# Token mix 2 in four steps between the pairs of channel product 1, and token mix 1 only inside channel product 2

## The chip, the cores and the metric

The kernel runs on one core of a Trainium2 chip. The metric is the device time of one execution in microseconds (us). The core's engines work in parallel, each through its own instructions in order: PE (TensorE, the matrix products), DVE (VectorE), ACT (ScalarE), POOL (GpSimd) and SP (SyncE, which here only issues transfers). Semaphores order them against each other.

## The reference

Eight batches of 4096 tokens by 192 channels, all in fp32. Cut to what matters:

```
w = softmax(weight, axis=-1)                              # 8 heads, 7 taps; a head is 24 channels
x = causal depthwise convolution of x with w              # along the tokens, per head
u = x + (relu(x^T @ w_tok1) @ w_tok2)^T                   # w_tok1 4096 x 256, w_tok2 256 x 4096
out = u + relu(u @ w_ch1) @ w_ch2                         # w_ch1 192 x 1536, w_ch2 1536 x 192
```

## The kernel before, in words

Work is done in five groups of batches: two of one batch (called single here) and three of two batches (pair groups). Group 0 is batch 0, group 1 batch 1, group 2 batches 2 and 3, and so on. Each batch has eight tiles of 512 tokens. A tile-batch, 64 of them in all, is numbered here as a *row*, from 1 on: rows 1 to 8 are batch 0, rows 9 to 16 batch 1, rows 17 to 32 group 2, rows 33 to 48 group 3.

Four kinds of matrix product share PE:

- **Token mix 1** (`mix`, line 861): `x^T @ w_tok1`, summed over all 4096 tokens of a group in two banks of the accumulator memory (`ps_a`). A group's tokens come in units called q, of two token rows each; a q needs `xhl` (the convolved tokens, split into a high and a low part by ACT, line 824, and DVE, line 828; two buffers) and a part of `w_tok1` (`t1`, loaded by SP and in group 2 split as well, lines 808 and 812).
- **Token mix 2** (`mix2`, line 1030): the next tile's `u`, four banks of `ps_x`, added to the convolved tokens on DVE (lines 1041 and 1042 for a single batch, 1051 for a pair).
- **Channel product 1** (`channel1`, line 1211): six pairs p of 18 matmuls. Each pair fills two banks of `ps_x`, which ACT (`hh`, line 1268) and DVE (`hl`, line 1269) read out.
- **Channel product 2** (`channel2`, line 1286): four banks of `ps_x`, read out by DVE (`osb`, lines 1298 and 1299).

`ps_x` has six banks in rotation. The operands stand in high and low parts, and three products of parts make one exact product. A matmul uses 64 of the 128 rows of the PE array, and two that stand next to each other run at the same time on the two halves, into different banks. Mix 1, mix 2 and product 2 need both halves for every bank, so they run in steps: halves 0 and 1 of the operands into two banks, and then the halves swapped:

```
SHARES = (0, 1), (2, 3), (1, 0), (3, 2)
```

Between a step and its swap `part_ends` (line 422) has ACT copy two zeros into the end of a bank: PE's next matmul into that bank waits for ACT, and ACT waited for PE's last one. I call it the handshake.

While a group's tiles run through mix 2 and both channel products, the next group is prepared in the background: its convolution (`taps`: DVE line 737, the first of seven taps on ACT), its loads and splits, and its mix 1. Class `Background` sets the order. It holds streams of items with a cost, a lag and a gate, and two clocks, `bg.pe` and `bg.dve`. At each `bg.fg(pe, dve, after)` in the code of the foreground the PE clock is advanced, and the items that are due, by these clocks, are written out at that place. What is left when a group ends is forced (`bg.finish`), and `bg.require(tag)` forces the items up to a tag and sets the PE clock to the later of the two. The clocks are a plan: on the chip each engine runs through its row as fast as its semaphores let it.

After mix 2 the next `u` must be transposed for the next product 1. Up to row 10 PE does that inside product 2. Later DVE transposes blocks of 32 x 32 (lines 1044 and 1052), and `blocks_sent` moves the blocks by 16 transfers, eight from SP's queue and eight from POOL's (line 1126). `parted_single` or `parted` then splits the result (ACT lines 1136, 1157 and 1162, DVE lines 1142 and 1159), and the next product 1 starts. SP's queue carries in the same order the loads of the raw tokens (`raw`, line 725), of `t1` (lines 789 to 802), of `w_tok2` (`t2`, line 979) and of `u` (line 986). From about 1320 us on there is no background left (rows 41 to 64, called quiet here).

Of the kernel before, what the change touches and what calls it, by code (L numbers as in the profile page):

```python
# [34 lines left out]
class Background:  # L35
# [112 lines left out]
def conv_mixer_kernel(ctx: ExitStack, tc: tile.TileContext, x, weight, w_tok1, w_tok2, w_ch1, w_ch2, out):  # L148
# [14 lines left out]
    MJ = 2  # L163
# [257 lines left out]
    def part_ends(ps):  # L421
        nc.scalar.copy(out=ps[0:1, TT - 2:TT], in_=seen)  # L422

# [278 lines left out]
    def stage1(gi, pools):  # L702
# [138 lines left out]

        def mix(q2, q, step):
            st = states[q2]
            n = q2 * (RB // MJ) + q
            if step == 0:
                st["full", q] = bg.full
            st["chunk", q] = bg.chunk
# [7 lines left out]
            else:  # L855
                kcs = (0, 1) if (n + step) % 2 == 0 else (1, 0)
# [8 lines left out]
                if step == 0:  # L865
                    part_ends(accs[kcs[1]])
# [3 lines left out]
        last_q = RB // MJ - 1  # L870
        def loaded(q2, part):
# [60 lines left out]
        for q2 in range(NS):  # L932
# [75 lines left out]
    def mix2(gi, q, t2, u, turned=None):  # L1008
        nb = len(GROUPS[gi])
        n = nb * D  # L1010
# [7 lines left out]
        if nb == 1:  # L1018
            prods = [(kc, r, h1[:, kc, :2 - r, :n], (2 - r) * D) for kc in range(KC) for r in range(2)]
        else:  # L1020
            prods = [(kc, r, h1[:, kc, v, :n], n) for kc in range(KC) for r, v in ((0, 0), (0, 1), (1, 0))]
        pss = {}
        for step, js in enumerate(SHARES):
            for j in js:
                if step < 2:
                    pss[j] = ps_x.tile([P, TT], F32, name="ps_x")
            for i, (kc, r, v, m) in enumerate(prods):
                for k, j in enumerate(js):
                    ks = half_rows(k)
                    nc.tensor.matmul(  # L1030
                        out=pss[j][:, :m], lhsT=lhs(kc, r, j)[ks], rhs=v[ks], start=step < 2 and i == 0,
                        stop=step > 1 and i == len(prods) - 1,
                    )
            if step < 2:
                part_ends(pss[js[1]])
            bg.fg(570 if nb == 1 else 1060, 0 if step < 2 else 1320 if nb == 1 else 1200, 200)
            for j in sorted(js) if step > 1 else ():
                ps = pss[j]
                if nb == 1:
# [3 lines left out]
                    if turned is not None:  # L1043
                        nc.vector.transpose(
                            out=turned[:, :D // QB, j * QB:(j + 1) * QB], in_=two.rearrange("p (n e) -> p n e", e=QB)
                        )
                        bg.dve += 380
                else:
                    uj = u[:, j]
# [535 lines left out]
```

## Time and profile before

| | us |
|---|---|
| three runs | 2056.75, 2057.18, 2061.10 (median 2057.18) |
| the profiled execution | 2053.17 |
| its span | 2051.4 |
| PE busy in the span | 2008.7 |
| DVE, ACT, POOL busy | 1370.7, 807.8, 219.1 |

The profiled execution is 4.0 us faster than the median of the runs. Its mean granted PE clock is 0.997 of full speed. The profile gives busy time by engine, groups of instructions by source line with the idle time before them and what ended it, waits, the chain of work that ended last, and a timeline of every instruction.

### The profile page before, as it was taken

How to read it: one execution, taken by the hardware profiler on the slowest of the kernel's cores; microseconds unless marked ns; L12 is line 12 of the kernel's file. 1: busy time of each engine (PE TensorE's matmuls, PEld its weight loads, DVE VectorE, ACT ScalarE, POOL GpSimd, SP SyncE). 2: the span in 40 equal slices, each digit the busy share in tenths (PEclk: the TensorE clock that was granted, in tenths of full speed). 3: DMA queues.
4: the chain of work that ended last, by engine and by line, in shares of the span. 5: the costliest groups of instructions: out<-in, count | busy, mean ns of one | idle time of the engine just before them, and what ended most of it. 6: DMA issues, size and time to landing. Idle time of an engine off the chain costs nothing.

```text
span 2051.4 us, 52173 instructions
## 1 busy us (share of the span) xinstructions
PE 2008.7 (98%) x22452; PEld 1889.9 (92%) x22452; DVE 1370.7 (67%) x2675; ACT 807.8 (39%) x1562; POOL 219.1 (11%) x385
## 2 busy tenths in 40 slices
PE   9999999998999999999999999999999999999999
PEld 8888999997989998998998989999999999999998
DVE  8888989888858879768745785444454444454443
ACT  5677534433333434334333343332332233333322
POOL 0000000021211011111111001111110111001110
PEclk9999999999999999999999999999999999999999
DMA  9955445656445777266634274322332333333320
GB/s 301 312 166 185 144 133 175 177 144 187 135 133 135 189 190 179 75 153 168 168 76 114 78 221 116 83 70 54 84 77 75 84 80 79 76 76 83 77 54 17
DMA packets 285237, 262.67 MB, mean 128 GB/s; under 512 B 189136, under 2 KB 233040, under 8 KB 285008
## 3 DMA queue, kind: packets, MB, share of 16 engines
q1 hardware_dynamic: 263280, 185.27, 33.6%
q0 software_dynamic: 21728, 74.08, 12.7%
q8 instruction: 177, 2.90, 0.6%
q14 instruction: 52, 0.43, 0.1%
HBM read 146.31 MB, written 71.30 MB: 106 GB/s over the span
## 4 chain that ended last, share of the span: by engine, by line
PE 76%; DVE 9%; DMA 6%; ACT 4%; SPq 3%; issue 1%; POOL 1%; ACTq 0%; DVEq 0%
PE ps_x L1211 34%; PE ps_x L1286 31%; PE ps_a L861 5%; PE ps_x L1030 4%; DVE xc L737 3%; DMA dec_raw<-in_moe_w_tok_dram 2%; DVE hl L1269 2%; SPq L1126 2%; DMA other<-own_hi 1%; DMA raw<-in_x_dram 1%; ACT own_hi L1157 1%; ACT other L1162 1%; DVE own_hi L1052 1%; POOL other L1126 1%; DVE u L1051 1%
## 5 line engine op out<-in xcount | busy, mean ns | idle before, releaser
L1286 PE MATMUL ps_x<-w,hh 64*128 64x384 f32 x5856 | 860.6, 357 | 0.3 <-DVE hl L1269 0.3
L1286 PE MATMUL ps_x<-w,hl 64*128 64x192 f32 x5856 | 831.7, 247 | 0.0
L1286 PEld LDWEIGHTS ps_x<-w,hl 64*128 64x128 f32 x5856 | 738.1, 188 | 0.1
L1286 PEld LDWEIGHTS ps_x<-w,hh 64*128 64x128 f32 x5856 | 734.2, 184 | 1.7 <-DVE hl L1269 0.8
L1268 ACT ACTIVATE hh<-ps_x 128x512 fp32r<-128x512 f32 x744 | 403.6, 594 | 565.8 <-PE ps_x L1211 565.7
L1269 DVE SCALAR_TENSOR_TENSOR hl<-ps_x,hh 128x512 fp32r<-128x512 f32 x744 | 477.1, 685 | 204.6 <-ACT hh L1268 203.6
L737 DVE SCALAR_TENSOR_TENSOR xc<-raw,cw,xc 128x384 f32<-128x384 f32 (+1 forms) x768 | 383.5, 562 | 18.6 <-ACT xc L735 18.5
L1211 PE MATMUL ps_x<-other,w_hi 64*128 64x512 f32 x1296 | 342.1, 390 | 12.6 <-ACT other L1162 12.6
L1211 PE MATMUL ps_x<-own_hi,w_hi 64*128 64x512 f32 x1440 | 338.8, 396 | 10.0 <-ACT own_hi L1136 8.8
L1211 PE MATMUL ps_x<-own_hi,w_lo 64*128 64x512 f32 x1440 | 331.6, 390 | 0.0
L1211 PE MATMUL ps_x<-own_lo,w_hi 64*128 64x512 f32 x1440 | 330.9, 390 | 0.0
L1211 PEld LDWEIGHTS ps_x<-other,w_hi 64*128 64x128 f32 x1296 | 235.5, 184 | 38.4 <-ACT other L1162 16.6
L1298 DVE TENSOR_TENSOR osb<-ps_x,u 128x192 f32<-128x192 f32 x244 | 85.6, 351 | 266.1 <-PE ps_x L1286 266.1
L1211 PEld LDWEIGHTS ps_x<-own_hi,w_hi 64*128 64x128 f32 x1440 | 216.0, 185 | 29.0 <-ACT own_hi L1136 10.2
L1211 PEld LDWEIGHTS ps_x<-own_hi,w_lo 64*128 64x128 f32 x1440 | 221.8, 186 | 18.2
L1211 PEld LDWEIGHTS ps_x<-own_lo,w_hi 64*128 64x128 f32 x1440 | 220.5, 185 | 18.7 <-ACT own_lo L1075 0.4
L422 ACT COPY ps_x<-seen 1x2 f32<-1x2 f32 x198 | 30.1, 152 | 393.1 <-PE ps_x L1286 331.3
L1211 PE MATMUL ps_x<-other,w_lo 64*128 64x512 f32 x648 | 182.8, 388 | 0.0
L1030 PE MATMUL ps_x<-h,t 64*128 64x384 f32 (+1 forms) x1408 | 134.6, 327 | 2.1 <-DVE hl L1269 1.8
L1030 PEld LDWEIGHTS ps_x<-h,t 64*128 64x128 f32 x1408 | 128.0, 184 | 5.2 <-DVE hl L1269 3.7
L1211 PEld LDWEIGHTS ps_x<-other,w_lo 64*128 64x128 f32 x648 | 119.4, 184 | 11.8
L861 PE MATMUL ps_a<-xhl,t 64*128 64x384 f32 x1080 | 123.6, 337 | 5.3 <-ACT ps_a L422 3.0
(176 smaller groups left out, 1826.4 us busy)
## 6 DMA issues: line engine op xcount, KB each, us to landing
raw<-in_x_dram SPq DMA_DIRECT2D x56, 672.0 KB, 8.1
t<-t2d SPq DMA_DIRECT2D x64, 512.0 KB, 5.9
u<-xcd SPq DMA_DIRECT2D x62, 384.0 KB, 7.5
xcd<-xc POOLq DMA_DIRECT2D x28, 768.0 KB, 7.8
t<-t1p SPq DMA_DIRECT2D x32, 512.0 KB, 5.0
out_dram<-osb POOLq DMA_DIRECT2D x34, 384.0 KB, 3.6
out_dram<-osb SPq DMA_DIRECT2D x29, 384.0 KB, 2.8
t2d<-stage SPq DMA_DIRECT2D x16, 512.0 KB, 4.4
```

The costliest lines, as they stand in the source:

```text
L422: nc.scalar.copy(out=ps[0:1, TT - 2:TT], in_=seen)
L737: nc.vector.scalar_tensor_tensor(out=dst, in0=src, scalar=cw[:, h, k:k + 1], in1=dst, op0=ALU.mult, op1=ALU.add)
L861: nc.tensor.matmul(out=accs[kcs[k]][:, :nb * D], lhsT=w[ks], rhs=x[ks], start=first and step == 0 and i == 0, stop=last and step == 1 and ...
L1030: nc.tensor.matmul(out=pss[j][:, :m], lhsT=lhs(kc, r, j)[ks], rhs=v[ks], start=step < 2 and i == 0, stop=step > 1 and i == len(prods) - 1,)
L1051: nc.vector.tensor_tensor(out=uj, in0=v, in1=uj, op=ALU.add)
L1052: nc.vector.transpose(out=turned[:, :, j * QB:(j + 1) * QB], in_=uj.rearrange("p c b d -> p (c b d)").rearrange("p (n e) -> p n e", e=QB),)
L1126: queue.dma_start(out=f32(home[q * QB:(q + 1) * QB, :, i * P:(i + 1) * P]), in_=blocks[i * QB:(i + 1) * QB, q % (2 * nb)],)
L1211: nc.tensor.matmul(out=ps, lhsT=w1[w][rows, t[h][2][c], p * P:(p + 1) * P], rhs=t[h][v][rows, c], start=a and n == 0, stop=z and n == len( ...
L1268: nc.scalar.activation(out=h["hh", f], in_=ps, func=AF.Relu)
L1269: nc.vector.scalar_tensor_tensor(out=h["hl", f], in0=ps, scalar=0.0, in1=f32(h["hh", f]), op0=ALU.max, op1=ALU.subtract)
L1286: nc.tensor.matmul(out=pss[j][:, :m], lhsT=h[part, f][ks, j * P:(j + 1) * P], rhs=w2[ks, f, :m], start=step < 2 and n == 0 and part == "hh ...
L1298: nc.vector.tensor_tensor(out=rows(osb[:, j]), in0=rows(ps[:, :D]), in1=tokens(u, i)[:, j], op=ALU.add)
```

## The change

Mix 2 is no longer one block behind product 1. It returns a function for a step and one for the transposes, and the main loop hands the four steps to `channel1` as `between`, in the order 0, 2, 1, 3. In most tiles they stand ahead of pairs 3, 4 and 5 and behind the last pair; inside a pair group (`at = 2`) ahead of pairs 2, 3, 4 and 5. So pairs of product 1 lie between a step and its swap. The adds follow the steps, the transposes follow product 1.

Mix 1 may start a step 0 only in the first half of product 2, and a step 1 only in its second half, where product 2 itself has already changed its banks (`bg.slot`); no zeros are copied for mix 1, except where steps are forced. Steps come in sets of q: two in the pair groups, four in the single one. Inside product 2 the planner's call comes one matmul group earlier (`n % 4 == 2`), with a further call at the end of a step, and PE's transposes of the single tiles start at (1, 5) instead of (1, 11). In batch 0 the `require` for `w_tok2` now falls between pairs 2 and 3 of product 1.

```diff
         def mix(q2, q, step):
...
             if step == 0:
-                st["full", q] = bg.full
-            st["chunk", q] = bg.chunk
+                st["full", q], done["slot"] = bg.full, bg.slot
+            elif not (st["full", q] or after_other()):
+                part_ends(last_bank[0])
...
-                kcs = (0, 1) if (n + step) % 2 == 0 else (1, 0)
+                kcs = (0, 1) if (n // some + step) % 2 == 0 else (1, 0)
...
-                if step == 0:
-                    part_ends(accs[kcs[1]])
+                last_bank[0] = accs[kcs[1]]
...
+        some = 2 if nb > 1 else last_q + 1
...
+        def after_other():
+            slots = done["slot"], bg.slot
+            return None not in slots and slots[1] >= slots[0] + 2
...
+        def multiply(q2, qs):
+
+            def ready(q):
+                n = q2 * (last_q + 1) + q
                 x = done.get(("split", q2, q) if nb > 1 else ("conv", q2))
-                return None if x is None else max(done["t1", n] + 4e3, x + 1200)
...
+                if x is None or not (bg.forced or bg.full or bg.slot is not None and bg.slot % len(SHARES) < 2):
+                    return None
+                return max(done["t1", n] + 4e3, x + 1200)
...
+            def other_step(q):
+                return 0.0 if bg.forced or states[q2]["full", q] or after_other() else None
 
             for step in range(2):
...
+                for q in qs:
+                    n = q2 * (last_q + 1) + q
+                    it = Item(lambda q=q, step=step: mix(q2, q, step), pe=MJ * (320 if nb == 1 else 520))
...
-            for q in range(0, last_q + 1, 2):
-
-                for k in range(2):
-                    prepare(q2, q + k)
-                for k in range(2):
-                    multiply(q2, q + k)
+            for q in range(0, last_q + 1, some):
+                qs = range(q, q + some)
+                for k in qs:
+                    prepare(q2, k)
+                multiply(q2, qs)
...
-    def mix2(gi, q, t2, u, turned=None):
+    def mix2(gi, q, t2, u):
...
+        def turn(z, js):
             for j in js:
...
+        def step(n):
+            js = SHARES[n]
...
-            bg.fg(570 if nb == 1 else 1060, 0 if step < 2 else 1320 if nb == 1 else 1200, 200)
+            bg.fg(570 if nb == 1 else 1060, 0 if n < 2 else 1320 if nb == 1 else 900, 200)
...
-        return {(1, NF - 1): lambda: turn(0), (2, 3): parts}
+        return {(1, 5): lambda: turn(0), (2, 3): parts}
...
-    def channel1(t, hold):
+    def channel1(t, hold, between):
...
             if p == hold:
                 bg.hold()
+            if p in between:
+                between[p]()
             pss = channel1_mm(t, p)
...
     def channel2(i, h, u, osb, between):
...
+                bg.slot = len(SHARES) * jobs[0] + step if n < NF - 1 else None
-                if n % 4 == 3:
-                    bg.fg(1140, 1320 if z else 0, 200)
+                if n % 4 == 2:
+                    bg.fg(1140, 0, 200)
+                if z:
+                    bg.fg(0, 1320, 200)
...
+                ahead = quiet and i == 0
+                step = None
+                if not plain and (ahead or turn and not ready):
+                    step, turned = mix2(*nxt, *loaded)
+                    at = 2 if turn and nb > 1 and nxt[0] == gi else 3
+
+                    def part(n):
+                        if gi == 0 and nxt[0] == 0 and n == 0:
+                            bg.require(("t2", nxt[1] // 2, nxt[1] % 2))
+                        step(n)
+
+                    parts = {at + k: lambda n=n: part(n) for k, n in enumerate((0, 2, 1, 3))}
                 if not plain:
-                    h = channel1(abc[i], (0 if pairs else NP) if by_blocks else None)
+                    h = channel1(abc[i], (0 if pairs else NP) if by_blocks else None, parts if step else {})
...
-                    if gi or q:
-                        mix2(*nxt, *loaded, turned=z)
+                    if step:
+                        for k, js in enumerate(((0, 1), (2, 3))):
+                            if k and NP in parts:
+                                parts[NP]()
+                            if z is not None:
+                                turned(z, js)
```

Where the instructions move is seen in each engine's order. Three places follow; the number behind `x` is how many such instructions stand in a row.

**PE, row 16, the last tile of batch 1** (`h_507` is mix 1's result, `t_8233` or `t_8213` the part of `w_tok2`, `w_1188` is `w_ch2`). Before, mix 2 stands in one piece between product 1 (line 1211) and product 2 (line 1286):

```order
L1211 MATMUL ps_x<-own_hi,w_hi 128x512 x6
L1211 MATMUL ps_x<-own_hi,w_lo 128x512 x6
L1211 MATMUL ps_x<-own_lo,w_hi 128x512 x6
L1030 MATMUL ps_x<-h_507,t_8233 128x384 x48
L1286 MATMUL ps_x<-w_1188,hh_8239 128x384 x2
```

After (product 1 is line 1227, mix 2 line 1055, product 2 line 1308):

```order
L1227 MATMUL ps_x<-own_lo,w_hi 128x512 x6
L1055 MATMUL ps_x<-h_507,t_8213 128x384 x12
L1227 MATMUL ps_x<-own_hi,w_hi 128x512 x6
L1227 MATMUL ps_x<-own_hi,w_lo 128x512 x6
L1227 MATMUL ps_x<-own_lo,w_hi 128x512 x6
L1055 MATMUL ps_x<-h_507,t_8213 128x384 x12
...
L1055 MATMUL ps_x<-h_507,t_8213 128x384 x12
L1308 MATMUL ps_x<-w_1188,hh_8219 128x384 x2
```

The 48 matmuls are now four sets of 12 with a pair of product 1 between each two.

**DVE, row 6, a tile of batch 0, the last pairs of product 1 and the adds of mix 2** (`hl` is the read-out of product 1, `xc` the taps; the DVE lines 1269, 737, 1041 and 1042 are 1287, 738, 1066 and 1067 after). Before:

```order
L1269 SCALAR_TENSOR_TENSOR hl_2876<-ps_x,hh_2875 128x512 x2
L737 SCALAR_TENSOR_TENSOR xc_2492<-raw_2459,cw,xc_2492 128x8x24 x2
L1269 SCALAR_TENSOR_TENSOR hl_2876<-ps_x,hh_2875 128x512 x2
L737 SCALAR_TENSOR_TENSOR xc_2492<-raw_2459,cw,xc_2492 128x8x24 x2
L1269 SCALAR_TENSOR_TENSOR hl_2878<-ps_x,hh_2877 128x512 x2
L737 SCALAR_TENSOR_TENSOR xc_2492<-raw_2459,cw,xc_2492 128x8x24 x2
L1269 SCALAR_TENSOR_TENSOR hl_2878<-ps_x,hh_2877 128x512 x2
L737 SCALAR_TENSOR_TENSOR xc_2492<-raw_2459,cw,xc_2492 128x8x24 x6
L1041 TENSOR_TENSOR u<-ps_x,u 128x192
L1042 TENSOR_TENSOR u<-ps_x,u 128x192
```

After:

```order
L1287 SCALAR_TENSOR_TENSOR hl_2858<-ps_x,hh_2857 128x512 x2
L219 TENSOR_TENSOR t2s<-dec_top,t2s 128x512
L738 SCALAR_TENSOR_TENSOR xc_2517<-raw_2442,cw,xc_2517 128x8x24 x8
L1287 SCALAR_TENSOR_TENSOR hl_2858<-ps_x,hh_2857 128x512 x2
L1066 TENSOR_TENSOR u<-ps_x,u 128x192
L1067 TENSOR_TENSOR u<-ps_x,u 128x192
L1066 TENSOR_TENSOR u<-ps_x,u 128x192
L1067 TENSOR_TENSOR u<-ps_x,u 128x192
L1287 SCALAR_TENSOR_TENSOR hl_2860<-ps_x,hh_2859 128x512 x2
```

Two taps behind every read-out of a pair have become a run of eight behind the read-out of pair 2, ahead of that of pair 3. Rows 3, 4 and 7 have the same (10, 8 and 10 taps).

**DVE, row 15, the forced rest of group 2's mix 1 behind product 2** (`osb` is product 2's read-out; lines 812 and 828 are 813 and 829 after). PE has there 96 matmuls of mix 1 in a row before and 192 after. Before:

```order
L1298 TENSOR_TENSOR osb<-ps_x,u 128x192
L1299 TENSOR_TENSOR osb<-ps_x,osb 128x192
L828 TENSOR_TENSOR xhl<-xc_6792,xhl 128x768
L812 TENSOR_TENSOR other<-other 128x2x256
L828 TENSOR_TENSOR xhl<-xc_6792,xhl 128x768
L812 TENSOR_TENSOR other<-other 128x2x256
L828 TENSOR_TENSOR xhl<-xc_6792,xhl 128x768
```

After:

```order
L1323 TENSOR_TENSOR osb<-ps_x,u 128x192
L1324 TENSOR_TENSOR osb<-ps_x,osb 128x192
L738 SCALAR_TENSOR_TENSOR xc_7287<-raw_6659,cw,xc_7287 128x16x24 x12
L813 TENSOR_TENSOR t_7468<-t_7468 128x2x256
L829 TENSOR_TENSOR xhl<-xc_5646,xhl 128x768
L813 TENSOR_TENSOR t_8006<-t_8006 128x2x256
L829 TENSOR_TENSOR xhl<-xc_5646,xhl 128x768
L813 TENSOR_TENSOR t_8021<-t_8021 128x2x256
L829 TENSOR_TENSOR xhl<-xc_7287,xhl 128x768
```

and three more such pairs. Twelve taps and six splits stand there now where three splits stood.

More of the change, by code (lines that the diff above doesn't have):

```diff
@@ L46, in __init__ @@
         self.forced = False
-        self.chunk = 0
+        self.slot = None
         self.pe = 0.0
@@ L1030, in mix2 @@
                     nc.tensor.matmul(
-                        out=pss[j][:, :m], lhsT=lhs(kc, r, j)[ks], rhs=v[ks], start=step < 2 and i == 0,
-                        stop=step > 1 and i == len(prods) - 1,
+                        out=pss[j][:, :m], lhsT=lhs(kc, r, j)[ks], rhs=v[ks], start=n < 2 and i == 0,
+                        stop=n > 1 and i == len(prods) - 1,
                     )
-            if step < 2:
+            if n < 2:
                 part_ends(pss[js[1]])
-            bg.fg(570 if nb == 1 else 1060, 0 if step < 2 else 1320 if nb == 1 else 1200, 200)
-            for j in sorted(js) if step > 1 else ():
+            bg.fg(570 if nb == 1 else 1060, 0 if n < 2 else 1320 if nb == 1 else 900, 200)
+            for j in sorted(js) if n > 1 else ():
                 ps = pss[j]
@@ L1042, in mix2 @@
                     nc.vector.tensor_tensor(out=two, in0=ps[:, :D], in1=one, op=ALU.add)
[L1043 to L1047, printed above, removed]
-                else:
-                    uj = u[:, j]
-                    v = ps[:, :n].rearrange("p (b c d) -> p c b d", b=nb, d=D2)
-                    nc.vector.tensor_tensor(out=uj, in0=v, in1=uj, op=ALU.add)
-                    nc.vector.transpose(
-                        out=turned[:, :, j * QB:(j + 1) * QB],
-                        in_=uj.rearrange("p c b d -> p (c b d)").rearrange("p (n e) -> p n e", e=QB),
-                    )
-                    bg.dve += 580
+                else:
+                    v = ps[:, :W].rearrange("p (b c d) -> p c b d", b=nb, d=D2)
+                    nc.vector.tensor_tensor(out=u[:, j], in0=v, in1=u[:, j], op=ALU.add)
+        return step, turn
     def own_tile(n):
@@ L1495, in conv_mixer_kernel @@
                 elif turn:
-                    if gi == 0 and nxt[0] == 0:
-                        bg.require(("t2", nxt[1] // 2, nxt[1] % 2))
                     z = up.tile([P, ND * NQ, P], F32, name="own_hi") if by_blocks else None
-                    if gi or q:
-                        mix2(*nxt, *loaded, turned=z)
+                    if step:
[4 more added lines that the diff above has]
+                                turned(z, js)
+                    elif q:
+                        if gi == 0 and nxt[0] == 0:
+                            bg.require(("t2", nxt[1] // 2, nxt[1] % 2))
+                        step, turned = mix2(*nxt, *loaded)
+                        for n in range(len(SHARES)):
+                            step(n)
                     else:
@@ L1517, in conv_mixer_kernel @@
                 end = last and q + 1 == NT and i + 1 == nb
-                if quiet and i == 0:
+                if ahead:
                     z = cps[0].tile([P, RB + HALO, 2, D // 2], F32, name="raw0")
                     z = z.rearrange("p r b d -> p (r b d)")[:, :ND * NQ * P].rearrange("p (n t) -> p n t", t=P)
-                    mix2(*nxt, *loaded, turned=z)
+                    for k, js in enumerate(((0, 1), (2, 3))):
+                        if k and NP in parts:
+                            parts[NP]()
+                        turned(z, js)
                     spare = not spare
```

54 lines of the change are left out of this document (31 added, 23 removed).

## The prediction

> **What bounds the kernel now.** I read the page's head first, then the windows by stage, the waits of PE, and the timeline around each wait.
>
> ```profile
> span 2051.4 us, 52173 instructions
> PE 2008.7 (98%) x22452; PEld 1889.9 (92%) x22452; DVE 1370.7 (67%) x2675; ACT 807.8 (39%) x1562; POOL 219.1 (11%) x385
> ```
>
> PE is busy for all but 42.7 us of the span, and the change leaves PE the same matmuls. So only three things can move the time: PE's gaps, stretches in which PE is granted half its clock, and new gaps. The windows (start:end, length, then busy time of PE, PE's weight loads, DVE, ACT and POOL, granted PE clock, DMA share, GB/s) say where the gaps lie; their limits are those of the groups, with the forced rest of mix 1 by itself.
>
> ```profile
> 110.00:330.00 220.00, 215.73 (x2472) 202.71 (x2472) 192.69 (x455) 131.49 (x252) 9.79 (x15) 1.00 0.52 156
> 330.00:565.00 235.00, 224.08 (x2568) 214.39 (x2568) 196.69 (x395) 92.27 (x198) 37.97 (x64) 0.98 0.58 169
> 565.00:581.00 16.00, 13.50 (x138) 11.12 (x137) 8.93 (x18) 5.99 (x14) 1.07 (x2) 1.00 0.75 229
> 581.00:1322.00 741.00, 723.05 (x8243) 676.60 (x8243) 534.65 (x1009) 275.61 (x536) 90.68 (x155) 1.00 0.52 135
> 1322.00:2040.00 718.00, 718.00 (x8218) 681.51 (x8215) 343.78 (x652) 233.99 (x449) 72.81 (x133) 1.00 0.30 74
> ```
>
> PE's gaps by window are 4.3, 10.9, 2.5, 18.0 and 0 us. The quiet third has none to win, and in the first window DVE is busy for 192.69 of 220 us, 0.88: that is where DVE can become the bound. PE's waits (us in all, times, longest) put names to the gaps:
>
> ```profile
> PE ps_x L1211 <- ACT other L1162: 12.6, 10, 2.0
> PE ps_x L1211 <- ACT own_hi L1136: 8.8, 2, 6.2
> PE ps_a L861 <- ACT ps_a L422: 6.6, 7, 2.7
> PE ps_a L861 <- DMA t<-t1p: 2.3, 1, 2.3
> PE ps_x L1030 <- DVE hl L1269: 1.8, 4, 1.3
> PE ps_x L1030 <- ACT ps_x L422: 1.1, 3, 0.4
> ```
>
> The chain in the quiet part gives the yardsticks (start, us, what, matmuls):
>
> ```profile
> 1363.95 13.58 PE ps_x L1286 x190
> 1377.53 12.45 PE ps_x L1211 x108
> ```
>
> A product 2 takes 13.58 us and a pair of product 1 12.45 / 6 = 2.08 us.
>
> **Gain 1: the two long waits for own_hi.** Timeline of PE, SP and ACT at the starts of rows 13 and 14:
>
> ```profile
> 458.74 1.83 PE L1211 MATMUL ps_x<-own_hi,w_hi 64*128 64x512 f32 x6 [2.62 <-ACT own_hi L1136]
> 462.46 0.85 PE L1211 MATMUL ps_x<-own_hi,w_hi 64*128 64x512 f32 x6
> 478.96 5.90 SPq L725 DMA_DIRECT2D raw<-in_x_dram  x2
> 485.17 9.69 SPq L1126 DMA_DIRECT2D own_lo<-own_hi  x8
> 498.69 1.66 ACT L1136 CAST own_hi<-own_lo 128x512 fp32r<-128x512 f32 x3 [11.51 <-DMA own_lo<-own_hi]
> 499.36 1.83 PE L1211 MATMUL ps_x<-own_hi,w_hi 64*128 64x512 f32 x6 [6.16 <-ACT own_hi L1136]
> 503.23 0.85 PE L1211 MATMUL ps_x<-own_hi,w_hi 64*128 64x512 f32 x6
> ```
>
> SP issues two loads of raw tokens and then the eight blocks, and issuing the blocks takes 9.69 us since SP waits among them; product 1 then waits 6.16. In the new order the raw loads follow the planner's calls inside product 1, two and a half to three pairs ahead of product 2, about 5 us earlier, and the `t1` loads that stood between raw and blocks stand behind the blocks. That covers 2.62 wholly and 6.16 nearly. Behind each wait the first 18 matmuls take 3.72 and 3.87 us instead of 2.08, which is PE at half clock: 1.6 and 1.8 more. Gain 2.62 + 6.16 + 3.4 = 12.2; the ends are 0 (the blocks' own landing sets the time) and 12.2. I take 12.2, since the shorter wait needs only half of those 5 us.
>
> **Gain 2: waits for L1162.** Ten waits, 12.6 us, 1.26 each. They come at tiles of the pair groups, where the transposed blocks come back late. In the new order five of these ten have 48 matmuls of mix 1 inside the product 2 ahead of the wait, which before lay elsewhere: 24 pairs x 0.174 = 4.2 us of cover (0.174 by the 24 matmuls, 12 pairs, that take 2.09 of the 2.19 us quoted under gain 4). Gain 5 x 1.26 = 6.3, ends 0 and 12.6.
>
> **Gain 3: mix 1's handshake and a load.** The handshake of mix 1 costs 6.6 us of waits; four of them, 0.25 + 3 x 0.30 = 1.15 us, lie in the forced stretch and stay. 5.45 go, because a step 1 now follows product 2's own swap. The 2.3 us wait for `t1` goes too, as mix 1 of group 3 starts its loads a half product 2 earlier than its matmuls; half clock behind it, estimated at the 1.7 of gain 1, as well. Sum 9.4, ends 4 and 9.4.
>
> **Gain 4: mix 2's handshake in the 13 single tiles, rows 3 to 15.**
>
> ```profile
> 236.52 2.19 PE L1030 MATMUL ps_x<-h,t2s 64*128 64x384 f32 x24
> 239.05 0.82 PE L1030 MATMUL ps_x<-h,t2s 64*128 64x384 f32 x8 [0.35 <-ACT ps_x L422]
> 239.71 0.36 PE L1286 MATMUL ps_x<-w,hh 64*128 64x384 f32 x2
> ```
>
> From the first matmul to product 2 it is 3.19 us. Its 16 pairs, half of them 384 and half 192 columns wide, need 8 x (0.174 + 0.087) = 2.09, so this tile loses 1.1. Thirteen such would be 14.3; what the list of waits shows is 1.1 + 1.8 = 2.9. I take the middle, 8.6. A pair of product 1 (2.08 us) now lies between step and swap, ACT's copy needs 0.15, so nothing of it is left.
>
> The gains sum to 12.2 + 6.3 + 9.4 + 8.6 = 36.5.
>
> **Cost 1: the forced rest of mix 1 in row 15, 192 matmuls instead of 96.** PE, DVE and ACT there, and ten taps of a pair group:
>
> ```profile
> 566.84 1.28 PE L861 MATMUL ps_a<-xhl,t 64*128 64x384 f32 x12
> 567.02 0.35 DVE L1298 TENSOR_TENSOR osb<-ps_x,u 128x192 f32<-128x192 f32 x1
> 569.65 0.95 DVE L828 TENSOR_TENSOR xhl<-xc,xhl 128x768 fp32r<-128x768 f32 x1
> 572.53 0.83 ACT L824 CAST xhl<-xc 128x768 fp32r<-128x768 f32 x1
> 572.66 0.69 DVE L812 TENSOR_TENSOR other<-other 128x512 fp32r<-128x512 f32 x1 [2.06 <-ACT other L808]
> 578.52 1.31 PE L861 MATMUL ps_a<-xhl,other 64*128 64x384 f32 x12 [0.30 <-ACT ps_a L422]
> 579.67 0.85 PE L1211 MATMUL ps_x<-own_hi,w_hi 64*128 64x512 f32 x6
> 657.98 5.34 DVE L737 SCALAR_TENSOR_TENSOR xc<-raw,cw,xc 128x384 f32<-128x384 f32 x10
> ```
>
> Before, the stretch lasts 579.67 - 566.84 = 12.83 us for 48 pairs x 0.174 = 8.35: 4.5 are lost. The matmuls more are no cost, as they are missing elsewhere. After, with E for product 2's end: two q are ready, and PE is through with both steps of them at E + 5.2 (8.35 / 2 and 1.0 of handshakes). DVE does half of `osb` by then due (2.63 / 2 = 1.3), twelve taps at 0.53 (6.4), one `t1` split (0.65) and one `xhl` split (0.95): E + 9.3, and with ACT and semaphores E + 9.75, so PE stands for about 4.55. Then three more sets of two q wait for a buffer of `xhl` to come free and be filled, 0.83 + 0.95 each, 5.3; handshakes 1.0. With 2 us of half clock behind the longest gap that is 12.9 lost, 8.4 more than before. Ends: 3 (the taps done earlier) and 14 (nothing of the splits beside PE). By the Trainium skill, "TensorE: Matmul & The Clock Gate", section "What's actually happening", the clock drops after at least one idle window of about 3.4 us and comes back after one busy window. By that rule the stretch would cost 1.7 rather than 2; the trace here had half clock already after 2.62 us.
>
> **Cost 2: 32 matmuls of group 1's mix 1 forced in row 7**, where none was. Four handshakes at 0.45 and a wait for `t1`, issued only about 3.4 us ahead:
>
> ```profile
> t<-t1d SPq DMA_DIRECT2D x29, 256.0 KB, 5.3
> ```
>
> 1.8 + 5.3 - 3.4 = 3.7; less a tenth or two for the matmuls that need no load, 3.3; ends 1 and 6.
>
> **Cost 3: runs of taps inside product 1, rows 3, 4, 6 and 7.**
>
> ```profile
> 235.34 1.29 DVE L1269 SCALAR_TENSOR_TENSOR hl<-ps_x,hh 128x512 fp32r<-128x512 f32 x2
> 238.56 2.06 DVE L737 SCALAR_TENSOR_TENSOR xc<-raw,cw,xc 128x192 f32<-128x192 f32 x6
> ```
>
> A tap takes 0.34. With T the end of pair 2 on PE, DVE ends `hl` of pair 2 at T + 1.9, a run of ten taps at T + 5.3 (eight and a decode are about the same), and `hl` of pair 3 at T + 6.9 with what lies between. Step 1 of mix 2 takes banks that this read-out frees, and PE is there at T + 0.52 + 2.08 + 0.52 + 2.08 = T + 5.2: it waits 1.7 or 1.8. The adds of step 2 then end 1.4 later, and pair 5 behind step 1 waits 0.85 for their banks. 2.6 in each of four tiles, 10.4; ends 0 (DVE ahead of the plan) and 34 (all 13 tiles, below). Other late read-outs: 2.
>
> The costs sum to 8.4 + 3.3 + 10.4 + 2.0 = 24.1, the net gain is 12.4. The quiet tiles I put at nothing: mix 2's banks come free there with all of product 2 to spare. The profiled execution would come to 2053.2 - 12.4 = 2040.8. The median of the runs is 4.0 above it, so I predict 2057.2 - 12.4 = 2044.8, rounded to 2044.
>
> **The rivals.** A measurement of this kernel can tell about 0.2% from no change: 2053.1 to 2061.3 is the same.
>
> *More is gained.* The taps of cost 3 find a DVE that has caught up by pair 2 (in the window 110 to 330 it stands idle for 27 us in all), and the twelve taps of cost 1 are done before E. Then 10.4 and 6.5 of the costs go: 2027. Against it: in those tiles 0.88 is an average, and the planner puts the run there because its clock of DVE is ahead.
>
> *No change.* The waits for own_hi stay, because the blocks' transfers and not the raw loads set them; 2044 + 12.2 = 2056. For it: the raw loads wait for a buffer that taps free, and DVE is no faster.
>
> *Slower: DVE's row behind mix 2's banks.* Product 1 now shares its six banks with mix 2, and PE's steps stand inside it, so any late `hl` stops PE, where before it had the four banks of product 2 as slack. If the 2.6 us come in each of the 13 single tiles, it is 33.8 instead of 10.4: 2067. It decides above 27.6 / 13 = 2.1 us a tile. For it: 0.88 in the first window. Against it: outside those four tiles the order of DVE there has no such run between these read-outs.
>
> *Slower: clock lost in the changed rhythm.* Short pauses at each change of banks, between pairs and steps, could take PE's clock down. The trace has a stretch with mix 1's steps set among other work:
>
> ```profile
> 530.00:567.00 37.00, 37.00 (x444) 37.00 (x442) 27.66 (x56) 14.56 (x30) 8.43 (x14) 1.00 0.56 176
> ```
>
> Its clock is 1.00 and PE has no gap. If each of the first 13 tiles lost 1.7, it would be 22 more: 2066. The same page of the Trainium skill, section "A second HAM failure mode: psum-queue depth-cycling", speaks for this rival: it tells of a kernel that cycled through accumulator banks and lost throughput to a clock that went up and down. This window does not agree with it.
>
> **How the numbers follow.** Forecast 0.47 (2035 to 2052), more gained 0.22, no change 0.16, DVE slower 0.12, clock 0.03. Faster is 0.47 + 0.22 = 0.69, the same 0.16, slower 0.15. The range reaches from 2026 (the costs absorbed) to 2058 (no change); the slower cases are left out, and a little below 2026.
>
> **What would show it.** Right: no wait of L1152's casts (L1136 before) over 2 us, no `ps_a` waits outside row 7 and row 15, no mix 2 handshakes, about 4 us waits of PE in the forced stretch, and waits of 1 to 2 us for `hl` or the `u` adds in rows 3, 4, 6 and 7. Wrong: these waits in all single tiles, or own_hi still late.

## The result: slower, and where the time went

The changed kernel takes 2089.49 us (median of 4 runs), the kernel before 2058.93 (4 runs): a ratio of 1.0143, 95% interval 1.012 to 1.0166. Ratios, here and below, are taken over all fast runs of both kernels, so they differ a little from the quotient of the medians, and one run of e7 at 5251.15 us is left out of its figures. I had forecast 2044. The profiled execution of after takes 2090.08 us, its span is 36.9 us longer than that of before.

The head of its page, and PE's waits (us in all, times, longest):

```profile
span 2088.3 us, 52085 instructions
PE 2034.3 (97%) x22452; PEld 1889.1 (90%) x22452; DVE 1359.1 (65%) x2675; ACT 802.8 (38%) x1510; POOL 218.3 (10%) x385
...
t<-t2d SPq DMA_DIRECT2D x64, 512.0 KB, 5.4
```

```profile
PE ps_x L1055 <- DMA t<-t2d: 19.9, 26, 1.9
PE ps_x L1227 <- ACT other L1178: 9.2, 7, 2.0
PE ps_a L867 <- DVE xhl L829: 7.2, 4, 5.9
PE ps_x L1055 <- DVE hl L1287: 3.5, 10, 0.8
PE ps_a L867 <- ACT ps_a L421: 2.0, 7, 0.3
...
PE ps_a L867 <- DMA t<-t1p: 1.2, 1, 1.2
...
PE ps_x L1055 <- ACT ps_x L421: 0.4, 1, 0.4
PE ps_x L1227 <- ACT own_hi L1173: 0.2, 1, 0.2
```

Beside the waits of before: those for own_hi at L1136 (8.8; L1152 in after) are gone, 0.2 is left at another line, and the handshakes of mix 1 and mix 2 nearly so (6.6 to 2.0, 1.1 to 0.4). L1162's are L1178's and down from 12.6 to 9.2. But the first line is new. Mix 2 waits 26 times for `t2`, the part of `w_tok2` that it multiplies by; before it waited for that not once. And the wait for `xhl`, whose largest part lies in the forced stretch, has grown from 1.3 to 7.2. On SP's queue the raw loads now stand 10.8 us ahead of the blocks of row 14 (6.2 in before, 478.96 to 485.17), and `t1` stands behind them:

```profile
470.85 1.26 SPq L726 DMA_DIRECT2D raw<-in_x_dram  x2
481.69 6.12 SPq L1142 DMA_DIRECT2D own_lo<-own_hi  x8
487.91 1.32 SPq L800 DMA_DIRECT2D t<-t1d  x2
```

The matmuls are the same in both kernels, so the start of a row's product 1 (its first matmul) can be set against that of the same row before. In us, minus is earlier than before; values from the two profiled executions, and in the same way for the experiments below:

| start of row | 3 | 9 | 15 | 16 | 33 | 41 | 64 |
|---|---|---|---|---|---|---|---|
| after | -1.5 | +9.4 | -4.8 | +13.0 | +19.5 | +12.4 | +37.1 |
| e1 (t2 loaded early) | -2.1 | +7.2 | -13.0 | +2.4 | +6.9 | -2.0 | +0.4 |
| e6 (e1, batch 0's mix 2 as before) | -0.1 | +1.4 | -19.0 | -3.4 | -2.0 | -9.8 | -7.6 |
| e7 (e1, no runs of taps) | -1.7 | +2.9 | -17.1 | -0.8 | +9.0 | +1.0 | +3.1 |
| e9 (mix 1's part alone) | -0.7 | +1.0 | -18.6 | -4.5 | -2.6 | -8.3 | -8.3 |
| e11 (before, raw loads held) | -2.3 | -2.4 | -10.6 | -10.7 | -10.2 | -8.6 | -8.6 |
| e12 (best) | -1.8 | -1.3 | -10.4 | -10.9 | -12.0 | -20.8 | -20.8 |

Rows differ in how much of mix 1 lies in them, so a step in this table is no loss by itself where mix 1 was moved across it. Row 15 has 192 matmuls of mix 1 in after and had 144 (48 in its product 2 and the 96 behind it): 24 pairs more, 4.2 us, which rows 9 to 14 have less. Rows 33 to 41 are to be read as one.

Two executions also differ by themselves: e11 has the order of before up to row 9 and is 2.3 us earlier at row 3, and from row 16 to 33, where e1, e6 and e7 have one order of instructions on DVE, ACT, SP and POOL, they lose 4.5, 1.4 and 9.8. Rows 3 to 9 repeat better (after, e2 and e4, with one order there, lose 10.9, 10.8 and 9.1), and so do the quiet rows (e1, e6, e7 and e8 lose 2.1 to 4.8).

From row 41 on there is no mix 1. There after loses 24.7 us in 23 quiet rows, the part of the kernel that I had put at nothing. The windows of these rows in before and in after (limits; length, PE, weight loads, DVE, ACT, POOL, clock, DMA share, GB/s):

```profile
1377.20:2021.80 644.60, 644.60 (x7434) 613.31 (x7432) 307.38 (x583) 208.74 (x401) 66.20 (x121) 1.00 0.30 74
```

```profile
1389.70:2058.90 669.20, 654.37 (x7436) 599.72 (x7434) 302.11 (x583) 208.21 (x401) 65.95 (x121) 0.99 0.29 71
```

PE had no gap there and has 14.8 us now. The other 9.8 us of the 24.6 are in PE's busy time, which counts matmuls by their modelled ends: two spells of half clock, 3.4 us each (from 1515.9 and from 1693.4, clock 0.50), account for 3.4 of them, and the rest I put down to the starts of short sets of matmuls behind each wait, which no view shows apart. One quiet tile, row 49. In before its product 1 starts at 1602.2; SP's queue and PE:

```profile
1604.00 0.36 SPq L1330 DMA_DIRECT2D out_dram<-osb  x1
1604.46 0.93 SPq L979 DMA_DIRECT2D t<-t2d  x2
```

```profile
1614.55 3.69 PE L1030 MATMUL ps_x<-h,t 64*128 64x384 f32 x39
```

In after it starts at 1625.0:

```profile
1626.66 0.36 SPq L1355 DMA_DIRECT2D out_dram<-osb  x1
1627.12 0.93 SPq L988 DMA_DIRECT2D t<-t2d  x2
...
1647.19 5.10 SPq L1142 DMA_DIRECT2D xc<-raw  x8
```

```profile
1631.01 0.39 PE L1227 MATMUL ps_x<-other,w_hi 64*128 64x512 f32 x1
1631.82 0.79 PE L1055 MATMUL ps_x<-h,t 64*128 64x384 f32 x6 [0.42 <-DMA t<-t2d]
1633.21 0.79 PE L1055 MATMUL ps_x<-h,t 64*128 64x384 f32 x6 [0.60 <-DMA t<-t2d]
```

In both kernels the load of `t2` stands on SP's queue behind the output store, and the store waits until DVE has read out product 2, 1.7 to 1.9 us into the next product 1. A load takes 5.4 us to land (median of its 64), so `t2` is there about 7.5 us after product 1's start. Mix 2 used to come at 12.45, 10.1 us behind the start of the load's issue (1614.55 - 1604.46); its first step now comes behind three pairs, at 3 x 2.08 = 6.2, and waits for each of the two halves of the load.

### The profile page after: what moved, and what is told of

Read it like the earlier page. It is cut to its first block, busy times and chain, and to the rows that moved or that the text cites. A ratio compares the mean times of both kernels' runs of the same rounds, so it can differ in the third digit from the quotient of the medians.

```text
span 2088.3 us, 52085 instructions
## 1 busy us (share of the span) xinstructions
PE 2034.3 (97%) x22452; PEld 1889.1 (90%) x22452; DVE 1359.1 (65%) x2675; ACT 802.8 (38%) x1510; POOL 218.3 (10%) x385
## 4 chain that ended last, share of the span: by engine, by line
PE 75%; DVE 11%; DMA 8%; SPq 3%; ACT 2%; issue 1%; ACTq 0%; POOL 0%; DVEq 0%; POOLq 0%
PE ps_x L1308 32%; PE ps_x L1227 29%; PE ps_a L867 5%; PE ps_x L1055 5%; DVE xc L738 4%; DMA t<-t2d 4%; DVE hl L1287 2%; SPq L1142 2%; DMA raw<-in_x_dram 1%; PE ps_a L496 1%; DMA t<-t1p 1%; DVE osb L1324 1%; PE ps_x L1259 1%; DVE osb L1323 1%; DMA other<-own_hi 1%
## 5 line engine op out<-in xcount | busy, mean ns | idle before, releaser
L1308 PE MATMUL ps_x<-w,hl 64*128 64x192 f32 x5856 | 813.5, 247 | 0.0
L1308 PEld LDWEIGHTS ps_x<-w,hl 64*128 64x128 f32 x5856 | 675.0, 188 | 0.7
L1308 PEld LDWEIGHTS ps_x<-w,hh 64*128 64x128 f32 x5856 | 671.1, 184 | 1.5 <-ACT ps_x L421 0.3
L1227 PE MATMUL ps_x<-other,w_hi 64*128 64x512 f32 x1296 | 354.4, 393 | 10.3 <-ACT other L1178 9.2
L1227 PE MATMUL ps_x<-own_hi,w_hi 64*128 64x512 f32 x1440 | 353.8, 398 | 2.9 <-DVE hl L1287 1.0
L1227 PE MATMUL ps_x<-own_lo,w_hi 64*128 64x512 f32 x1440 | 345.0, 392 | 0.0
L1227 PE MATMUL ps_x<-own_hi,w_lo 64*128 64x512 f32 x1440 | 344.3, 391 | 0.0
L1227 PEld LDWEIGHTS ps_x<-own_hi,w_lo 64*128 64x128 f32 x1440 | 232.0, 186 | 19.9
L1227 PEld LDWEIGHTS ps_x<-own_lo,w_hi 64*128 64x128 f32 x1440 | 231.7, 186 | 20.1 <-ACT own_lo L1091 0.4
L1055 PE MATMUL ps_x<-h,t 64*128 64x384 f32 (+1 forms) x1408 | 160.0, 332 | 21.1 <-DMA t<-t2d 19.9
L1055 PEld LDWEIGHTS ps_x<-h,t 64*128 64x128 f32 x1408 | 139.1, 185 | 38.4 <-DMA t<-t2d 16.5
```

The costliest lines, as they stand in the source:

```text
L1055: nc.tensor.matmul(out=pss[j][:, :m], lhsT=lhs(kc, r, j)[ks], rhs=v[ks], start=n < 2 and i == 0, stop=n > 1 and i == len(prods) - 1,)
L1227: nc.tensor.matmul(out=ps, lhsT=w1[w][rows, t[h][2][c], p * P:(p + 1) * P], rhs=t[h][v][rows, c], start=a and n == 0, stop=z and n == len( ...
L1308: nc.tensor.matmul(out=pss[j][:, :m], lhsT=h[part, f][ks, j * P:(j + 1) * P], rhs=w2[ks, f, :m], start=step < 2 and n == 0 and part == "hh ...
```

## The experiments

**e1 and e2: is it the load, or the new rhythm of pairs and steps?** e1 issues the load before product 2; mix 2 has read the old `t2` by then.

```diff
...
+                early = load_t2(nxt[0], nxt[1] + 1, sp) if gi and turn and nxt[1] + 1 < NT else None
                 if plain:
                     first_channel2(...)
...
-                        loaded = load_tile(nxt[0], nxt[1] + 1, sp)
+                        loaded = load_tile(nxt[0], nxt[1] + 1, sp, early)
```

> The changed kernel with one thing different: outside batch 0 the next tile's w_tok2 part (t2) is loaded before product 2 instead of behind the output store that follows product 2; mix 2 has already read the old one by then. Theory load: the slowdown is mix 2, now 4 to 6 us into product 1, waiting for t2, which SP issues only behind the output store (26 waits of 19.9 us in the list, some 27 us with the ramps, two spells of half clock 3 us). Expected 2060 us, no waits of mix 2 for t<-t2d, quiet rows back to 26.0 and 30.4 us each. Rival rhythm: the pauses at the changes between pairs of product 1 and steps of mix 2 cost the time, and the load only shows as the last to arrive. Expected 2085 to 2090, waits of mix 2 taken over by hl or the copy. Rival traffic: the load moved into product 2 delays the blocks, waits for L1178's successor grow by what is won; 2075 to 2090.

Measured: 2055.77 us (10 runs) against 2054.88 of before, ratio 1.0005 (0.9989 to 1.002). After was 1.43% above before, so about 28 of its 29 us are back (the medians are 34 apart, but were taken in two sessions, in which before itself differed by 4). SP's queue in e1's row 49, mix 2's wait for `t2` in its list of waits, and its quiet rows:

```profile
1622.77 5.10 SPq L1146 DMA_DIRECT2D xc<-raw  x8
1627.97 1.06 SPq L987 DMA_DIRECT2D t<-t2d  x2
```

```profile
PE ps_x L1059 <- DMA t<-t2d: 1.0, 1, 1.0
```

```profile
1375.20:2022.20 647.00, 645.98 (x7435) 617.72 (x7432) 302.13 (x583) 208.59 (x401) 65.97 (x121) 1.00 0.30 72
```

The load now goes out behind the blocks, 36.7 us ahead of its use (mix 2 takes it at 1664.63). The quiet rows have 22.2 of the 24.6 us back, with the steps of mix 2 still between the pairs: it is the load, not the rhythm. What the remaining 2.4 us are was not traced. L1178's successor waits 9.0 us as against 9.2, so the rival of traffic falls too. e2 takes the quiet tiles alone back to the old place:

```diff
-                if not plain and (ahead or turn and not ready):
+                if not plain and turn and not ready:
...
+                    late, turned = mix2(*nxt, *loaded)
+                    for n in range(len(SHARES)):
+                        late(n)
...
```

> The changed kernel, but in the quiet tiles (no background left) mix 2 stands in one piece behind product 1, as before. Theory load and rival rhythm both expect the 33 us that rows 40 to 64 lost to come back, 2057 us; 8 us of t2 waits in rows 11 to 15 stay. If only part comes back, something else than the place of mix 2 slows the quiet tiles.

Measured: 2065.42 us, ratio 1.0049 (1.0034 to 1.0064), by the ratios 19 us below after, and 0.1 us less than before between rows 41 and 64. I expected 33 us back, which counted row 40 to 41, a place where mix 1 was moved and nothing was lost. Seven waits for `t2` are left in e2's list, 7.0 us.

**e3 and e9: the two halves of the change apart.** e3 keeps mix 2's move with mix 1 placed as before (`part_ends` behind each step 0, chunks in place of slots, sets of two q); e9 keeps mix 1's placement with mix 2 in one piece behind product 1 everywhere.

```diff
-                if not plain and (ahead or turn and not ready):
+                if False:          # e9; mix2 then runs all four steps behind product 1
...
```

> The changed kernel's mix 2 with the placement of mix 1 from before: steps of mix 1 anywhere, a copy of zeros behind each step 0, no slots. 96 matmuls are forced in row 15 instead of 192. Theory: the forced stretch gives back about 11 us, waits for the copy and for t1 (some 14 us) return, the quiet part stays at 33 us lost; 2088 to 2095. Rival: mix 1's new placement is the larger cost (the planner's order of taps goes with it); 2070 to 2080.

> The changed kernel with mix 2 behind product 1 in one piece everywhere, as before: what is left of the change is the new placement of mix 1 and the planner's calls. With e3 (mix 2 moved, mix 1 as before, 47 us above before) this closes the square. Theory additive: mix 2's move costs about 33 us in the quiet tiles, 8 us of t2 waits in rows 11 to 15 and 8 us in batch 0, so this kernel should lie 40 to 45 us below the changed one, about 2045, 10 us faster than before. Rival: mix 1's placement only pays together with mix 2's; then 2060.

Measured: e3 2102.07 us, ratio 1.023 (1.0202 to 1.0258), slower than either theory; e9 2041.48, ratio 0.993 (0.9907 to 0.9953). So mix 2's move costs 47 us, mix 1's new placement gains 14, and the sum, 33, is about what both together cost (1.0143 x 2055 - 2055 = 29, 25 to 34). Both kernels keep the change's new calls of the planner inside product 2, so these count in either half and were not tried alone. That e3 is worse than after lies largely in the same load: mix 2 waits 30.6 us for it in e3's list, against 19.9 (and mix 1 waits 8.2 us for ACT's copy, against 2.0). SP and PE of e3 in row 14:

```profile
500.64 5.10 SPq L1144 DMA_DIRECT2D own_lo<-own_hi  x8
...
506.48 3.72 SPq L728 DMA_DIRECT2D raw<-in_x_dram  x2
514.27 0.59 SPq L1357 DMA_DIRECT2D out_dram<-osb  x1
514.90 4.04 SPq L990 DMA_DIRECT2D t<-t2d  x2
```

```profile
524.55 0.85 PE L1057 MATMUL ps_x<-h,t 64*128 64x384 f32 x4 [6.51 <-DMA t<-t2d]
```

The two parts of the load take 4.04 us to issue there, and PE goes on 9.65 us after the issue began, with the raw loads just ahead on the queue; in the quiet tile above it is 0.93 and 6.1 us (1633.21 - 1627.12).

**e6 and e7: batch 0.** In e1 rows 3 to 9 still lose 9.3 us. e6 puts mix 2 of batch 0 back behind product 1; e7 leaves it between the pairs, and puts the planner's jump of `bg.pe` behind product 1, so that the runs of taps are gone.

```diff
-                if not plain and (ahead or turn and not ready):
+                if not plain and (ahead or turn and not ready and (gi or nxt[0])):      # e6
...
+                            was = bg.pe                                                 # e7
                             bg.require(("t2", nxt[1] // 2, nxt[1] % 2))
+                            bg.pe = was
...
+                    if step and gi == 0 and nxt[0] == 0:
+                        bg.pe = max(bg.pe, bg.dve)
```

> e1_t2_early with mix 2 of batch 0 (rows 3 to 7) in one piece behind product 1 again. In e1 rows 3 to 8 stand 9 us later against before than at their start. Theory: most of that is mix 2 inside product 1 of batch 0 (DVE late with its read-outs, banks not free), and 3 us are the 32 forced matmuls. Expected 6 us below e1, 2049, rows 4 and 5 as before. Rival: it is mix 1's new placement in batch 0 (four q at once, steps only inside product 2); then it stays at e1's 2055.

> e1_t2_early with mix 2 inside product 1 in batch 0, but the jump of the planner's PE clock that the requirement for w_tok2 makes is put behind product 1. The runs of 8 and 10 taps between the read-outs of pairs 2 and 3 are gone from DVE's order; from row 8 on nothing is changed. Theory taps: those runs cost 2 us in each of rows 3, 4, 6 and 7; expected 6 to 8 us below e1, 2048, no waits of mix 2 for hl over 0.4 us in these rows. Rival banks: six banks shared by product 1 and mix 2 stop PE whatever DVE does in between; within 2 us of e1.

Measured: e6 2045.42 us, ratio 0.9954 (0.994 to 0.9968); e7 2049.59 (nine runs), ratio 0.9977 (0.9962 to 0.9992). Between rows 3 and 9 e1 loses 9.3, e7 4.6, e6 1.5. So the runs of taps cost 4.7 us in four tiles, and mix 2 inside product 1 costs 3.1 more without them; e7's waits for `hl` stay up to 0.4 us. Both theories hold a part. A run of taps in after, row 7, with DVE's row first and PE's behind it:

```profile
269.15 3.38 DVE L738 SCALAR_TENSOR_TENSOR xc<-raw,cw,xc 128x192 f32<-128x192 f32 x10
272.45 1.29 DVE L1287 SCALAR_TENSOR_TENSOR hl<-ps_x,hh 128x512 fp32r<-128x512 f32 x2
```

```profile
273.19 0.44 PE L1055 MATMUL ps_x<-h,t2s 64*128 64x384 f32 x1 [0.76 <-DVE hl L1287]
273.79 0.82 PE L1055 MATMUL ps_x<-h,t2s 64*128 64x384 f32 x7 [0.16 <-DVE hl L1287]
```

**e4, e8 and e10: the forced stretch of row 15.** PE there in after:

```profile
562.47 3.32 PE L867 MATMUL ps_a<-xhl,t 64*128 64x384 f32 x26 [0.24 <-ACT ps_a L421]
571.70 3.89 PE L867 MATMUL ps_a<-xhl,t 64*128 64x384 f32 x22 [5.91 <-DVE xhl L829]
```

DVE does the twelve taps from 563.75 to 570.2 meanwhile, and PE comes back at half clock; the window's clock is 0.85, and the half clock lies between 567.0 and 577.2:

```profile
560.00:595.00 35.00, 26.27 (x215) 21.16 (x213) 20.24 (x36) 10.22 (x24) 5.00 (x8) 0.85 0.66 215
```

```profile
563.60:567.00 3.40, 2.12 (x18) 1.23 (x14) 3.40 (x8) 1.45 (x3) 0.00 (x0) 1.00 0.60 154
567.00:577.20 10.20, 5.20 (x30) 4.70 (x32) 6.12 (x10) 1.50 (x3) 2.87 (x4) 0.50 1.01 284
```

e4 (on e1) takes mix 1's stream ahead of the convolution's when a group is finished; e8 (on e7) and e10 (on e9) make the planner count a tap of group 2 at 0.8 of its cost.

```diff
-            for s in mine:
+            for s in reversed(mine):                                                    # e4
...
-            pace = PACE if gi == 1 and q2 + 1 < NS else 1.0
+            pace = PACE if gi == 1 and q2 + 1 < NS else 0.8 if gi == 2 else 1.0         # e8, e10
```

> e1_t2_early, and at the end of a group the forced rest takes the stream of mix 1 before the stream of the convolution, so that two splits stand ahead of the twelve taps on DVE in row 15. Theory taps: PE's wait of 5.9 us there, and the half clock behind it, come from the taps; a part of both goes: 5 to 8 us below e1. Rival: the stretch is bound by the two buffers of xhl in any order; within 2 us of e1.

> e7_t2_jump_late with the planner's cost of a tap of group 2 at 0.8 of its value, so that the convolution of group 2 is written out earlier: no tap stands behind product 2 of row 15, and 144 matmuls of mix 1 are forced there instead of 192. Theory taps: the wait of 5.9 us and most of the half clock behind it go; row 15 loses about 8 us less than in e7. Rival buffers: the two buffers of xhl and the copies set the stretch; then only the 48 matmuls move elsewhere and the total stays within 2 us of e7. Earlier taps can also delay read-outs in rows 10 to 14.

> e9_mix1_only with the planner's cost of a tap of group 2 at 0.8 of its value: no tap stands behind product 2 of row 15, 144 matmuls are forced there instead of 192. In e8 the same edit was worth nothing since mix 2 inside product 1 then waited for the load of u; here mix 2 stands behind product 1. Theory taps: the wait of 4.8 us in the forced stretch and the half clock behind it go, 5 to 7 us below e9, 2035. Rival buffers: the two buffers of xhl set the stretch; within 2 us of e9, 2041. Rival loads: the raw loads that go with earlier taps delay the blocks or u, own_hi waits return; 2045 and more.

Measured: e4 2062.05 us, ratio 1.003 (1.0016 to 1.0044), 6 us above e1; e8 2063.9, ratio 1.0045 (1.0031 to 1.0059), 14 above e7; e10 2045.99, ratio 0.9955 (0.9943 to 0.9968), not below e9 but about 5 us above it. My theory of a simple gain fell each time. In e4 a split of `t` that waits for PE now stands ahead of the taps:

```profile
567.85 0.69 DVE L813 TENSOR_TENSOR t<-t 128x512 fp32r<-128x512 f32 x1 [5.40 <-ACT t L809]
568.46 6.43 DVE L738 SCALAR_TENSOR_TENSOR xc<-raw,cw,xc 128x384 f32<-128x384 f32 x12
```

The stretch begins at 550.58 in e4, so the taps start 17.9 us into it instead of 3.8 (563.75 - 559.93 in after), and PE waits for them all the same, 6.43 us ahead of 575.86. In e10 the taps are gone from the stretch, and the wait for `xhl` falls from 6.1 to 3.6 us in all, but from row 9 to 15 e10 gains only 10.7 us where e9 gains 19.6, with as many matmuls (the 48 that are forced no more stand in row 15's product 2). PE's gaps in rows 9 to 14 are 5.0 us in e10 and 0.2 in e9: one wait of mix 2 for `t2` in row 13 has 2.3 of them, short waits for DVE's read-outs 2.5. e8 shows what an earlier step of a planner asks of the loads. The raw loads go out earlier, the store and the load of `u` stand behind them on SP's queue, and DVE's adds of mix 2, now in the middle of product 1, wait for `u`, with every read-out behind them:

```profile
462.40 6.23 SPq L726 DMA_DIRECT2D raw<-in_x_dram  x2
468.73 2.48 SPq L1359 DMA_DIRECT2D out_dram<-osb  x1
471.26 1.40 SPq L999 DMA_DIRECT2D u<-xcd  x1
```

```profile
478.00 0.36 DVE L1070 TENSOR_TENSOR u<-ps_x,u 128x192 f32<-128x192 f32 x1 [6.48 <-DMA u<-xcd]
```

```profile
478.89 1.36 PE L1231 MATMUL ps_x<-own_hi,w_hi 64*128 64x512 f32 x3 [5.90 <-DVE u L1071]
```

The wait of 5.9 us and the half clock of 6.8 us from 478.0 on, which loses 3.4, are 9.3 of the 18 us by which rows 9 to 15 of e8 are slower than those of e7; the rest I have not broken down.

**e11: the waits for own_hi, from the kernel before.** One expression of before is changed; raw loads then stand behind the eight blocks.

```diff
-                    h = channel1(abc[i], (0 if pairs else NP) if by_blocks else None)
+                    h = channel1(abc[i], 0 if by_blocks else None)
```

> The kernel before with one thing different: in the single tiles whose u is transposed by blocks, loads of raw tokens are held until the blocks are split, as in the pair groups; on SP's queue they stand behind the eight blocks instead of ahead of them. Theory queue: the two waits for own_hi (8.8 us and 3.4 of half clock) come from the raw loads directly ahead of the blocks; expected 12 us below before, 2044. Rival landing: the blocks' own landing sets the wait; within 2 us of before. Rival taps: raw tokens that arrive later delay the taps, more matmuls wait in rows 13 to 15; slower than before.

Measured: 2044.18 us against 2056.62, ratio 0.9941 (0.9928 to 0.9954), 12 us; in the profiled execution 8.2 of them lie between rows 9 and 15. SP's queue ahead of row 14 of e11:

```profile
480.06 5.09 SPq L1126 DMA_DIRECT2D own_lo<-own_hi  x8
485.20 2.65 SPq L725 DMA_DIRECT2D raw<-in_x_dram  x2
```

Issuing the blocks takes 5.09 us instead of 9.69 behind the raw loads, and the list has one wait for own_hi of 1.2 us.

**e12 and e13: the parts that pay, together.** Mix 2 behind product 1, the raw loads held, mix 1 only inside product 2 for groups 3 and 4 (e13: group 4 alone) and as before for groups 1 and 2, which keeps the forced stretch at 96 matmuls.

```diff
...
+        some, inside = 2, gi > 2            # e13: gi > 3; "inside" chooses the new rules of mix 1, else the old
...
```

> Parts put together: mix 2 in one piece behind product 1; raw loads held behind the blocks (e11); mix 1 of groups 1 and 2 placed as before (96 matmuls forced in row 15), mix 1 of groups 3 and 4 only inside product 2, as in the change. Theory parts add: 12 us from the queue (e11), in rows 33 to 41 the 6 us that e9 showed, in rows 17 to 33 e9's loss of 2: 2056 - 12 - 6 + 2 = 2040. Rival: the parts overlap (e9's 14 us contain the 12 already, and nothing else is won): 2044.

> e12 with mix 1 of group 3 placed as before too, so that only group 4's is kept inside product 2. Theory: rows 17 to 33 are as before, so 2 us below e12, 2038. Rival: rows 17 to 33 gain from the new placement here, as their first product 1 waits less; 2 us above e12.

Measured: e12 2032.18 us against 2055.08, ratio 0.9889 (0.9876 to 0.9903), 8 us better than expected; e13 2038.46, ratio 0.9911 (0.9896 to 0.9927). e12 beats before, after and e9. PE's waits in e12:

```profile
PE ps_x L1234 <- ACT other L1185: 5.6, 6, 2.0
PE ps_a L870 <- ACT ps_a L423: 3.9, 6, 1.8
PE ps_x L1062 <- DVE hl L1294: 1.9, 5, 1.3
```

It was e13 that I expected to be the better one; group 3's placement, which I took for a loss of 2 from e9's rows 17 to 33, is no loss. In the profiles e12 gains 1.1 there (from -10.9 to -12.0) and e13 loses 2.7, but that is within what one order of instructions differs by in these rows, so the size of it is not shown.

## Why the prediction was wrong, point by point

- **The step that failed: "The quiet tiles I put at nothing: mix 2's banks come free there with all of product 2 to spare."** I asked who waits for what mix 2 writes, and not what mix 2 reads. It reads `t2`, whose load stands behind the output store on SP's queue. Moving mix 2 from 12.45 to 6.2 us behind product 1's start takes away the time in which that load landed. e1 shows its size: about 28 us by the ratios, 22 of them in the quiet tiles. No rival of mine had it. The slower rival I named, DVE's row behind mix 2's banks, was on the right side (2067), but it came to 7.8 us in batch 0 and nowhere else.
- **The rest of the sum was off too, by 13 us.** With the load out of the way e1 stands at before's time, not 12.4 us below it. By the points below gains 2, 3 and 4 gave 2.9, 2.0 and 8.6 less and cost 1 took 3.1 more; costs 2 and 3 took 1.8 and 5.7 less; mix 2 in batch 0 took 3.1, where I had 2 for other late read-outs, and the quiet rows still lose 2.4. That adds up to 12.6, from single executions, so such an agreement is partly luck.
- **Gain 1** (12.2) was right in mechanism: the raw loads went out earlier, `t1` went behind the blocks, the waits at L1136 (8.8 us) are gone, and e11 gets 12 us from the place of the raw loads alone. It was the one large gain of this change. It does not come with mix 1's placement alone: neither e9 nor e3, where mix 1 is placed as before, has these waits, and in both the raw loads of row 14 stand behind the blocks. What the two share are the planner's new calls inside product 2; that they set this order is likely, but was not tried by itself.
- **Gain 2** (6.3) was 3.4 in after (12.6 to 9.2), and 6.4 in e9 (6.2 left), where mix 2 is not moved. Its price of 0.174 us for a pair was worked out wrongly: half of the 24 matmuls quoted under gain 4 are 192 columns wide. It holds for pairs of 384 columns (23 matmuls of mix 1 take 2.30 us at the start of after's forced stretch).
- **Gain 3** (9.4): the waits for ACT's copy fell by 4.6 of the 5.45, the load of `t1` still waits 1.2 of 2.3, and the half clock behind it (1124.1 to 1127.5 in before) is gone; with the 1.7 put for that, 7.4. Rows 33 to 41 give 7.1 us in after and 8.8 in e12.
- **Gain 4** (8.6) did not come. The handshake's wait fell by 0.7 us, but mix 2's wait for `hl` rose from 1.8 to 3.5. e6 and e9 differ in mix 2's place outside batch 0 and in the early load, and e6 is not the faster one (2045 and 2041). The 8.6 was the middle between 2.9, which the waits showed, and 14.3, which counted one tile's 1.1 us thirteen times; that 1.1 was also too large, since a set of 384 columns and one of 192 together take 0.28 to 0.29 us (from 239.71 to 239.99 to 240.28 in product 2 behind it), so that 16 pairs need 2.3 and not 2.09.
- **Cost 1** (8.4) was about 11.5: the forced stretch lasts 592.66 - 559.93 = 32.73 us for 96 pairs x 0.174 = 16.7, so 16.0 are lost against 4.5. The sum itself had left out the first 1.0 of handshakes (4.55 + 5.3 + 1.0 + 1.0 + 2 = 13.9, not 12.9). The rest is that DVE, still at the split of `own_lo` when product 2 ended at 560.1, began `osb` at 561.1 and the taps at 563.75, so that PE stood 5.9 us and not 4.55, and that half clock lasted 10.2 us, which loses 5.1 and not 2. Half clock was granted from 1.2 us into that wait on (567.0), behind a window of 3.4 us in which PE had been busy for 2.12. The section "What's actually happening" of the Trainium skill's page "TensorE: Matmul & The Clock Gate" puts half clock after at least one idle window of about 3.4 us. The wait of 5.9 us is longer than that, but the drop 1.2 us into it does not agree, and the trace decides.
- **Cost 2** (3.3) was about 1.5: three handshakes of 0.5, between the starts of matmuls in row 7's forced steps, and no wait for `t1d`.
- **Cost 3** (10.4) was 4.7 by e7; the place and the wait for `hl` were right, the size was twice too large: the longest wait is 0.8 us and not 1.7. Mix 2 in product 1 of batch 0 costs 3.1 besides.
- **The rival of rhythm** falls: e1's quiet rows have steps between pairs, a clock of 1.00 and 1.0 us of gaps in 647, and from 110 to 558 us, up to the forced stretch, its clock is 1.00 too. The section "A second HAM failure mode: psum-queue depth-cycling" of the same page of the Trainium skill tells of a kernel that lost throughput in such a rhythm; e1 does not agree with it.

What stays open: why e12 is 8 us better than the sum of its parts (it differs from before in the planner's calls inside product 2 too), and which part of the change sets the order of the raw loads. Neither was tried by itself.

## What to carry to other kernels

Before a step is moved earlier, list what it reads, and for each input the transfer that brings it, the queue that this stands on, and what stands ahead of it there; a load that was never seen waiting may have been covered by just the time that the move takes away. A planner's order also sets the order of the DMA queues: the same raw loads cost 12 us just ahead of the blocks and next to nothing behind them. And where a change has two halves, build each alone; here one half was worth 14 us and the other cost 47.
